# Where the last stage's weights are split: float32 kept during the attention, high and low halves made in the experts' stage

## The chip, the cores and the metric

One core of a Trainium2 chip runs the whole program in one launch. The metric is the device time of one execution in microseconds (us), the median of three runs. The engines are TensorE (PE, and PEld for its weight loads), VectorE (DVE), ScalarE (ACT), GpSimd (POOL), and SyncE (SP), which only issues DMAs.

## The reference

Three stages follow one another on 4 x 576 tokens of width 512:

```python
# 1. attention, 8 heads of 64, per batch
scores = scale * q @ k.T
scores = where(scores >= max(scores) - tau, scores, -1e9)
attn = exp(scores - max(scores)); attn /= sum(attn) + 1e-9
x = attn @ v                                   # heads side by side: 512 columns
# 2. experts: each token goes to one of 8 (fresh argmax, or that of the token before)
h = relu(x[b, s] @ w1[e])                      # w1: 8 x 512 x 1024
out[b, s] = p[e] * (h @ w2[e])                 # w2: 8 x 1024 x 512
# 3. feed-forward
xn = (x - mu) / sqrt(var + 1e-6) * g_ln
y = x + relu(xn @ w_ch1) @ w_ch2               # w_ch1: 512 x 2048, w_ch2: 2048 x 512
```

`w_ch1` and `w_ch2` come as float64. Products are wanted to float32 accuracy, and the kernel gets them from float16 matmuls: each operand is split into a high half (its float16 rounding) and a low half (what is left, in float16), and three products of halves are summed.

## The kernel before

**Order of the work.** Every engine takes its instructions in the order in which the code is written; nothing rearranges them. Waits between engines are semaphores, and an engine whose next instruction waits holds up all that stand behind it.

**Attention.** There are 16 pairs of heads with 9 items (row tiles of 128) each. Per item PE makes the scores (L399), DVE takes their maximum (L403), PE makes scores with the threshold added (L436, L441), ACT takes the exponential `e` (L446), DVE masks it into `em` (L452), ACT rounds the high half `hl` (L458), POOL subtracts to get the low half (L459), and PE multiplies by `v` (L474 to L478). Beside this, each pair's `q`, `k`, `v` are scaled and split (ACT L297, L305, L357, L362; POOL L306, L363), and POOL prepares the thresholds (L412 to L416). A table (`later`, filled by `at(item, step)`) puts background steps between the items.

**Weights of the last stage, first part.** Slots 0 to 10 of the 16 into which `w_ch1` and `w_ch2` are cut are converted during the attention, two halves (`a` = 0, 1) of 128 x 512 each, by `ffn_steps`. A half takes six steps at the offsets in `FO`: a DMA of the float64 words (L161), three DVE instructions that build the float32 (`narrow`, L142 to L146, into tile `cv`), a scaling on ACT (L164), and `low()`: ACT rounds the high half into `fw` (L157) and POOL subtracts for the low half (L158). `fw1` and `fw2` hold both halves for the whole program. Slots 11 to 15 are converted later by `ffn_half`, on ACT (L179) and DVE (L180).

**Experts.** The units are "a" and "b" (experts 0 and 1, two token tiles each), then 2 to 7 (two tiles of 128 tokens each), then 6 units whose expert is read from a register. A unit gathers its tokens (POOL, L904), transposes them (PE L987, ACT L988, DVE L989: tile `xT`), makes the hidden layer in four steps `k` (PE L1012, ACT L1016, DVE L1017: tile `hid`), then two output tiles (PE L1033, ACT L1039), and POOL scatters them (L1040, L1041). Between the steps `pace` runs the splits of the next unit's weights, eight chunks of 128 x 1024: high on ACT (L124), low on DVE (L125). In unit "b" DVE also makes the tables for the later units (L825 to L872, POOL L867).

**Feed-forward.** Nine groups of 256 tokens: PE L1144 and L1157 read `fw1` and `fw2`.

Of the kernel before, what the change touches and what calls it, by code (L numbers as in the profile page):

```python
# [8 lines left out]
F32 = mybir.dt.float32  # L9
# [3 lines left out]
AF = mybir.ActivationFunctionType  # L13
ALU = mybir.AluOpType
# [6 lines left out]
def kernel(  # L21
# [15 lines left out]
    nc = tc.nc  # L37
# [15 lines left out]
    def pool(c, name, bufs, **kw):  # L53
        return c.enter_context(tc.tile_pool(name=name, bufs=bufs, **kw))
# [65 lines left out]
    fw1 = fw_p.tile([128, 2, DM // 128, FF], F16, name="fw1")  # L120
    fw2 = fw_p.tile([128, 2, FF // 128, DM], F16, name="fw2")
# [5 lines left out]
    FA = 11  # L127

    def ffn_views(j):

        if j < 8:
            c, o = j // 2, 1024 * (j % 2)
            src = w_ch1[128 * c:128 * c + 128, o:o + 1024].rearrange("p (a b) -> p a b", a=2)
            return src, fw1[:, :, c, o:o + 1024].rearrange("p t (a b) -> p t a b", a=2), g32[:, c:c + 1]
        j -= 8
        src = w_ch2[256 * j:256 * j + 256, :].rearrange("(c p) f -> p c f", p=128)
        return src, fw2[:, :, 2 * j:2 * j + 2, :], 64.0

    def narrow(t, r):

        lo, hi = t[..., 0], t[..., 1]
        nc.vector.tensor_scalar(out=r, in0=hi, scalar1=3, scalar2=0x3FFFFFF8, op0=ALU.logical_shift_left, op1=ALU.bitwise_and)  # L142
        yield
        nc.vector.scalar_tensor_tensor(out=r, in0=hi, scalar=-(1 << 30), in1=r, op0=ALU.bitwise_and, op1=ALU.bitwise_or)
        yield
        nc.vector.scalar_tensor_tensor(out=r, in0=lo, scalar=29, in1=r, op0=ALU.logical_shift_right, op1=ALU.bitwise_or)  # L146
        yield

    def ffn_steps(j, a, cv_p):

        src, dst, scale = ffn_views(j)
        t = cv_p.tile([128, 512, 2], I32, name="stg")
        r = cv_p.tile([128, 512], I32, name="cv")
        rf = r.bitcast(F32)

        def low():
            nc.scalar.activation(out=dst[:, 0, a], in_=rf, func=AF.Copy)  # L157
            nc.gpsimd.tensor_tensor(out=dst[:, 1, a], in0=rf, in1=dst[:, 0, a], op=ALU.subtract)  # L158

        n = narrow(t, r)  # L160
        yield nc.sync.dma_start(out=t.rearrange("p b w -> p (b w)"), in_=src[:, a].bitcast(I32))  # L161
        for _ in range(3):
            yield next(n)
        yield nc.scalar.activation(out=rf, in_=rf, func=AF.Copy, scale=scale)  # L164
        yield low()

    def ffn_half(j, a):

# [15 lines left out]
    P, wt = {}, {}  # L184
# [45 lines left out]
    if True:  # L230
# [292 lines left out]
        def gate(p):  # L523

            b, hp = divmod(p, NP)
            xc = xcs[p]
            xt = xts[p % 2]
            ta = bank(b)
            for i in range(4):
                nc.tensor.transpose(ta[:, i, :], xc[:, i, :], ident)  # L530
            yield
            nc.scalar.activation(out=xt[:, 0:4, :], in_=ta, func=AF.Copy)
            close()
            yield
            tt = bank(b)
            nc.tensor.transpose(tt[:, 0, 0:64], xc[0:64, 4, :], ident[0:64, 0:64])
            yield
            nc.scalar.activation(out=xt[:, 4, 0:64], in_=tt[:, 0, 0:64], func=AF.Copy)
            close()
            yield  # L540
            lp = bank(b).rearrange("p a b -> p (a b)")[:, 0:80].rearrange("p (a b) -> p a b", b=16)
            for i in range(5):
                nc.tensor.matmul(lp[:, i, 0:9], xt[:, i, :], wg9[:, hp, :])
                if i % 2 and p < npair - 1:
                    yield
            yield
            lg = lgs[b % 2]
            if hp == 0:
                nc.vector.tensor_copy(out=lg, in_=lp[:, :, 0:9])
            else:  # L550
                nc.vector.tensor_tensor(out=lg, in0=lp[:, :, 0:9], in1=lg, op=ALU.add)
            close()
            if hp == NP - 1:
                if b < B - 1:
                    routes.append([route(b), None])
                else:
                    yield
                    yield from route(b)
# [177 lines left out]
        def at(k, f, *a):  # L736
            later.setdefault(max(-FIRST, k), []).append((f, a))
# [15 lines left out]
        for p in range(npair):  # L753
# [9 lines left out]
                at(9 * p + 10 + 4 * a, start_norm, p, a)  # L763
            at(9 * p + 15 + (4 if p == npair - 2 else 1 if p < npair - 2 else 0), store, p)
            at(9 * p + (17 if p < npair - 1 else 15), lambda p=p: bgp.append(gate(p)))
        FO = ((-4, 2, 3, 5, 5, 8), (0, 6, 9, 8, 8, 13))
        for w, slot in enumerate((0, 1, 2, 3, 4, 5, 7, 8, 9, 11, 12)):
            for a in range(2):
                g = []
                def st(w=w, a=a, g=g):  # L770
                    if not g: g.append(ffn_steps(w, a, cv_p))
                    next(g[0], None)
                for o in FO[a]:
                    at(max(-1, 9 * slot + o), st)
# [115 lines left out]
    def tiles(u):  # L890

        if u in PAIRS:
            return PAIRS[u]
        return (2 * u, 2 * u + 1) if u < E else (E + u,)

    def single(u):
        return u not in PAIRS and u >= E

    def gather(u):
        us[u, "g"] = []  # L900
        for n, c in enumerate(tiles(u)):
            xg = P["xgs"][u % 2 if single(u) else n]
            ix, R = (etb, NT - S) if u == "a" else (P["tb"], NT)
            nc.gpsimd.indirect_dma_start(  # L904
                out=xg[:], out_offset=None, in_=x_d[0:R, :], in_offset=bass.IndirectOffsetOnAxis(ap=ix[:, c:c + 1], axis=0),
                bounds_check=R - 1, oob_is_err=False)
            us[u, "g"].append(xg)
# [31 lines left out]
    def drip(n=1):  # L939

        if late:
            next(late.pop(), None)
        for _ in range(n):
            for k in pq:
                if k[0] == 1 and "wb_p" not in P:
                    return
                if k in parts and (not late if k[0] == "f" else k[0] < 2 or (k[0] - 2, k[1] // 4) in done):
                    break
                if k[0] != "f":
                    return  # L950
            else:
                return
            pq.remove(k)
            if k[0] == "f":
                late.append(parts.pop(k))
                next(late[0])
            else:
                parts.pop(k)()
            more()

    def pace(u, share):

        n = 0
        for k in pq:
            if k[0] != "f" and (k[0] - u) * 8 + k[1] > (7 if u < 6 else 11):
                break
            n += 1
        drip(int(n * share + 0.99))
# [8 lines left out]
    def new_x(u):  # L977
        us[u, "x"] = P["u_p"].tile([128, 2, 2, 4, 128], F16, name="xT")

    def t_unit(u):  # L980

        new_x(u)
        x = us[u, "x"]
        for n, xg in enumerate(us.pop((u, "g"))):
            t = P["pa"].tile([128, 4, 128], F32, name="a")
            for c in range(4):
                nc.tensor.transpose(t[:, c, :], xg[:, 128 * c:128 * c + 128], ident)  # L987
            nc.scalar.activation(out=x[:, 0, n], in_=t, func=AF.Copy, scale=64.0)  # L988
            V.scalar_tensor_tensor(out=x[:, 1, n], in0=t, scalar=64.0, in1=x[:, 0, n], op0=ALU.mult, op1=ALU.subtract)  # L989
# [55 lines left out]
    def s1_unit(u, k):  # L1045
        for _ in s1_steps(u, k):
            pass

    def s2_unit(u, i, between):
        for _ in s2_steps(u, i, between):  # L1050
            pass
# [18 lines left out]
    def f_load(g):  # L1070
        xf = P["f_p"].tile([128, 2, DM + 1], F32, name="xf", bufs=2)
        nc.sync.dma_start(out=xf, in_=ys_d[256 * g:256 * g + 256, :].rearrange("(t p) d -> p t d", p=128))
        fs[g] = xf
# [111 lines left out]
    with tc.manual_schedule():  # L1185
# [121 lines left out]
        for _ in ew: pass  # L1307
        t_unit("b")
        gather(2)
        for u in ["b"] + list(range(2, E)):  # L1310
            v = 1 if u == "b" else u
            for k in range(4):
                s1_unit(u, k)
                pace(v + 1, SH[k])
                for _ in range(3 if u == "b" else 1):
                    next(ut, None)
            t_unit(v + 1)
            gather(v + 2)
            if u == E - 1:
                gather(v + 3)  # L1320
            s2_unit(u, 0, lambda: pace(v + 1, SH[4]))
            if u == 2:
                dyn_tables()
                c_unit.close()
                c_tab.close()
                P["f_p"] = pool(ctx, "f", 1)
                P["f2_p"] = pool(ctx, "f2", 2)
            s2_unit(u, 1, lambda: pace(v + 1, SH[5]))
        f_load(0)
        for i in range(ND0):  # L1330
            u = E + i
# [76 lines left out]
```

## Time and profile before

| | |
|---|---|
| median of 3 runs | 1051.86 us (1051.25 to 1055.43) |
| the profiled execution | 1051.45 us, of which the span from first to last instruction is 1049.7 us |
| PE, DVE, ACT, POOL busy in the span | 990.2, 652.8, 505.1, 392.8 us |
| mean granted clock of PE | 0.988 |
| attention, pairs 1 to 14 | 54 to 376 us of the span |
| unit "b", unit 2, units 3 to 6 | 438 to 461, 461 to 484, 484 to 592 us |

Busy shares over the whole span mix stages with different limits, so each stage is read by itself: the windows table gives the busy time of every engine in a stretch. In the timeline a time in square brackets is the engine's idle time just before the instruction and what ended it; an instruction without brackets followed the one before it. A busy PE is not PE at its peak, since the ends of its matmuls are modelled.

### The profile page before, as it was taken

Reading aid. Unit: us, or ns where it says so; the run is one execution under the profiler, and the core shown is the slowest. Engines: PE = TensorE matmul, PEld = TensorE weight load, DVE = VectorE, ACT = ScalarE, POOL = GpSimd, SP = SyncE. Lnnn points to the kernel's source line nnn. Section 1 sums busy time; section 2 is a strip of 40 time slices with the busy share of each in tenths; the row PEclk is TensorE's granted clock in tenths of the full one; section 3 lists DMA queues with packets and bytes.
Section 4 is the critical chain, followed back from the end, with each engine's and each line's share of the span. In section 5 each row is a group of like instructions: output and inputs, shape, how many; then the busy total and the mean of one; then the engine's idle time right before and its main releaser. Section 6 shows DMA issues by size and latency. Waiting matters only on the chain. (4 is left out here: it accounts for less than half of the span.)

```text
span 1049.7 us, 23757 instructions
## 1 busy us (share of the span) xinstructions
PE 990.2 (94%) x9946; PEld 728.9 (69%) x9946; DVE 652.8 (62%) x1127; ACT 505.1 (48%) x791; POOL 392.8 (37%) x411
## 2 busy tenths in 40 slices
PE   6899998998999988899999999999999999999995
PEld 3678877787888776676667677594858668567572
DVE  7788888988897777797787777363324133131220
ACT  4688786786777666356566554242212011011010
POOL 3699897797788671334222211101000000000000
PEclk8999999999999999999999999999999999999998
DMA  7556544464442646668889775363111110111100
GB/s 179 138 133 166 132 103 126 112 156 119 113 108 47 166 153 213 214 217 278 268 290 304 239 251 164 105 200 106 38 31 40 52 32 31 54 28 41 31 11 23
DMA packets 122454, 136.83 MB, mean 130 GB/s; under 512 B 65370, under 2 KB 86874, under 8 KB 122336
## 3 DMA queue, kind: packets, MB, share of 16 engines
q1 hardware_dynamic: 98336, 116.43, 38.3%
q0 software_dynamic: 4960, 14.17, 3.7%
q10 hardware_dynamic: 19040, 4.61, 2.1%
q8 instruction: 80, 1.31, 0.5%
q14 instruction: 38, 0.31, 0.1%
HBM read 100.17 MB, written 19.94 MB: 114 GB/s over the span
## 5 line engine op out<-in xcount | busy, mean ns | idle before, releaser
L1144 PE MATMUL a<-nT,fw 128*128 128x256 f16 x1728 | 190.3, 273 | 0.8 <-DVE nT L1113 0.8
L459 POOL TENSOR_TENSOR hl<-em,hl 128x576 f16<-128x576 f32 x128 | 169.5, 1325 | 54.0 <-ACT hl L458 52.8
L1157 PE MATMUL y<-fw,hid 128*128 128x512 f16 x864 | 187.9, 379 | 0.0
L1144 PEld LDWEIGHTS <-fw 128*128 128x128 f16 x1728 | 169.1, 98 | 22.4 <-issue 0.9
L1157 PEld LDWEIGHTS <-hid 128*128 128x128 f16 x864 | 84.6, 98 | 100.4
L1147 ACT ACTIVATE hid<-a 128x512 f16<-128x512 f32 x72 | 42.7, 593 | 213.2 <-PE a L1144 211.3
L125 DVE SCALAR_TENSOR_TENSOR w<-stg,w 128x1024 f16<-128x1024 f32 x112 | 135.2, 1231 | 15.7 <-ACT w L124 14.8
L446 ACT ACTIVATE e<-s,t 128x576 f32<-128x576 f32 x144 | 106.0, 736 | 70.2 <-PE s L441 57.6
L1162 POOL DMA_INDIRECT out_dram<-xf x18 | 19.1, 1059 | 311.8 <-DVE xf L1161 311.8
L1012 PE MATMUL a<-xT,w 128*128 128x128 f16 (+1 forms) x1536 | 121.4, 241 | 1.4 <-DVE w L125 0.9
L1033 PE MATMUL y<-w,hid 128*128 128x512 f16 x528 | 117.8, 379 | 3.0 <-DVE hid L1017 2.7
L1012 PEld LDWEIGHTS <-w 128*128 128x128 f16 x1536 | 112.2, 99 | 11.1 <-DVE w L125 1.0
L403 DVE TENSOR_REDUCE mc<-sm 128x1 f32<-128x576 f32 x138 | 103.6, 751 | 24.7 <-PE sm L399 22.7
L124 ACT ACTIVATE w<-stg 128x1024 f16<-128x1024 f32 x112 | 114.4, 1051 | 6.1 <-DMA stg<-in_moe_w_dram 3.5
L452 DVE SCALAR_TENSOR_TENSOR em<-s,e 128x576 f32<-128x576 f32 x144 | 107.1, 745 | 9.7 <-POOL hl L459 8.5
L1148 DVE SCALAR_TENSOR_TENSOR hid<-a,hid 128x512 f16<-128x512 f32 x72 | 49.6, 688 | 98.9 <-ACT hid L1147 98.9
L1161 DVE SCALAR_TENSOR_TENSOR xf<-y,xf 128x512 f32<-128x512 f32 x18 | 12.5, 692 | 146.8 <-PE y L1157 146.8
L399 PE MATMUL sm<-qkt 128*128 128x288 f16 (+1 forms) x308 | 75.4, 291 | 24.3 <-DVE mc L403 21.4
L458 ACT ACTIVATE hl<-em 128x576 f16<-128x576 f32 x128 | 86.9, 679 | 18.8 <-DVE em L452 18.3
L1033 PEld LDWEIGHTS <-hid 128*128 128x128 f16 x528 | 51.0, 98 | 62.2 <-DVE hid L1017 4.5
L436 PE MATMUL s<-qkt 128*128 128x288 f16 (+1 forms) x320 | 90.2, 290 | 3.8 <-DVE em L452 3.1
L441 PE MATMUL s<-th,ind 128*128 128x128 bf16 (+5 forms) x960 | 91.9, 206 | 0.0
(295 smaller groups left out, 1800.4 us busy)
## 6 DMA issues: line engine op xcount, KB each, us to landing
stg<-in_moe_w_dram SPq DMA_DIRECT2D x112, 512.0 KB
stg<-in_moe_w_ch_dram SPq DMA_DIRECT2D x32, 512.0 KB
ys_d<-stg SPq DMA_DIRECT2D x6, 769.5 KB
xf<-ys_d SPq DMA_DIRECT2D x9, 513.0 KB
x_d<-xc SPq DMA_DIRECT2D x16, 256.0 KB
ku<-qkt SPq DMA_DIRECT2D x28, 144.0 KB
rawq<-in_q_dram SPq DMA_DIRECT2D x7, 512.0 KB
rawk<-in_k_dram SPq DMA_DIRECT2D x7, 512.0 KB
```

Of the source, the lines that this page charges most:

```text
L124: nc.scalar.activation(out=dst[:, 0, n], in_=t, func=AF.Copy, scale=scale)
L125: nc.vector.scalar_tensor_tensor(out=dst[:, 1, n], in0=t, scalar=scale, in1=dst[:, 0, n], op0=ALU.mult, op1=ALU.subtract)
L403: nc.vector.tensor_reduce(out=mcs[p % 2][:, j:j + 1], in_=mms.pop((p, j))[:, W0:W0 + 576], op=ALU.max, axis=AX.X)
L436: mm(o[:, W0 + 288 * c:W0 + 288 * c + 288], (kt, ku)[k][:, n], y, start=(k == 0), stop=False)
L441: mm(o[:, W0 + i:W0 + i + w], ind[:, t % 4, 0:o.shape[0]], y, start=False, stop=(i == of[-1][0]))
L446: nc.scalar.activation(out=e, in_=mst[p, j][:, W0:W0 + 576], func=AF.Exp, bias=t0, scale=SC)
L452: nc.vector.scalar_tensor_tensor(out=em, in0=ps[:, W0:W0 + 576], scalar=0.0, in1=e, op0=ALU.is_ge, op1=ALU.mult)
L459: nc.gpsimd.tensor_tensor(out=hl[:, 1], in0=em, in1=hl[:, 0], op=ALU.subtract)
L1012: nc.tensor.matmul(ps[:, f, :], t1[:, a, c, fc], x[:, h, i:i + N // 128, c, :], start=(n == 0), stop=(n == 11))
L1033: nc.tensor.matmul(ps, hid[:, x, f, 128 * i:128 * i + 128], t2[:, a, f, :], start=(n == 0), stop=(n == 23))
L1144: nc.tensor.matmul(ps[:, f, :], fw1[:, a, c, fc], x[:, h, :, c, :], start=(n == 0), stop=(n == 11))
L1157: nc.tensor.matmul(ps, hid[:, x, f, ts_], fw2[:, a, f, :], start=(n == 0), stop=(n == 47))
```

## The change

`low()` goes from the attention. ACT's scaling step (now L179 of the new file, L164 before) writes its float32 result to the bytes of `fw1` or `fw2` that the two halves will take: 512 float32 need as many bytes as 512 high and 512 low float16. In the experts' stage `ffn_finish` makes the halves of a slot in two parts: two copies on POOL into a float32 tile `f16`, then two roundings on ACT and two subtractions on POOL. One part is issued after each of the four hidden steps of units "b" and 2 to 7, until the 22 parts are done, which is in unit 6.

```diff
+    def ffn_whole(j, a):
+
+        c = j // 2
+        if j < 8:
+            o = 512 * (j % 2) + 256 * a
+            return fw1.bitcast(F32)[:, :, c, o:o + 256]
+        return fw2.bitcast(F32)[:, :, 2 * (j - 8) + a, :]
+
+    def ffn_finish(j):
+
+        dst = ffn_views(j)[1]
+        r = P["n_p"].tile([128, 2, 512], F32, name="f16", tag="f16")
+        for a in range(2):
+            nc.gpsimd.tensor_copy(out=r[:, a].rearrange("p (t f) -> p t f", t=2), in_=ffn_whole(j, a))
+        yield
+        for a in range(2):
+            nc.scalar.activation(out=dst[:, 0, a], in_=r[:, a], func=AF.Copy)
+        for a in range(2):
+            nc.gpsimd.tensor_tensor(out=dst[:, 1, a], in0=r[:, a], in1=dst[:, 0, a], op=ALU.subtract)
+        yield
+
     def ffn_steps(j, a, cv_p):
...
-        rf = r.bitcast(F32)
-
-        def low():
-            nc.scalar.activation(out=dst[:, 0, a], in_=rf, func=AF.Copy)
-            nc.gpsimd.tensor_tensor(out=dst[:, 1, a], in0=rf, in1=dst[:, 0, a], op=ALU.subtract)
-
+        rf = r.bitcast(F32).rearrange("p (t f) -> p t f", t=2)
         n = narrow(t, r)
         yield nc.sync.dma_start(out=t.rearrange("p b w -> p (b w)"), in_=src[:, a].bitcast(I32))
         for _ in range(3):
             yield next(n)
-        yield nc.scalar.activation(out=rf, in_=rf, func=AF.Copy, scale=scale)
-        yield low()
+        yield nc.scalar.activation(out=ffn_whole(j, a), in_=rf, func=AF.Copy, scale=scale)
...
-        FO = ((-4, 2, 3, 5, 5, 8), (0, 6, 9, 8, 8, 13))
+        FO = ((-4, 2, 3, 5, 5), (0, 6, 9, 8, 8))
...
         gather(2)
+        fin = (x for j in range(FA) for x in ffn_finish(j))
         for u in ["b"] + list(range(2, E)):
             v = 1 if u == "b" else u
             for k in range(4):
...
                 for _ in range(3 if u == "b" else 1):
                     next(ut, None)
+                next(fin, None)
             t_unit(v + 1)
...
+        for _ in fin: pass
         f_load(0)
```

On POOL in the attention, from the split of one pair's `v` (`vl`) to the split of the next pair's `q` (`nat`), before:

```order
L363 TENSOR_TENSOR vl_164<-vraw,vh_163 128x640
L459 TENSOR_TENSOR hl<-em,hl 128x576
L158 TENSOR_TENSOR fw_96<-cv,fw_96 128x512
L459 TENSOR_TENSOR hl<-em,hl 128x576
L459 TENSOR_TENSOR hlt<-em,hlt 128x576
L459 TENSOR_TENSOR hl<-em,hl 128x576
L306 TENSOR_TENSOR nat<-rawq,nat 128x9x64
```

The same stretch in the changed kernel, whose line numbers are 15 higher there:

```order
L378 TENSOR_TENSOR vl_164<-vraw,vh_163 128x640
L474 TENSOR_TENSOR hl<-em,hl 128x576 x2
L474 TENSOR_TENSOR hlt<-em,hlt 128x576
L474 TENSOR_TENSOR hl<-em,hl 128x576
L321 TENSOR_TENSOR nat<-rawq,nat 128x9x64
```

The subtraction into `fw` is gone, and all else keeps its place; it is so at all 22 places, and on ACT with the rounding L157. The order on PE, DVE and SP is the same in both kernels throughout.

On POOL from the gathers for unit 2 (`xg`) to the first output of unit "b" (`yb`), before:

```order
L904 DMA xg_7409<-x_d,tb 128x512
L904 DMA xg_7410<-x_d,tb 128x512
L867 TENSOR_TENSOR ova<-oca,val_79 128x1280
L904 DMA xg_7409<-x_d,tb 128x512
L904 DMA xg_7410<-x_d,tb 128x512
L1040 COPY yb<-tb 128x1
L1041 DMA ys_d<-yb,didx 2304x513
```

And in the changed kernel (`f_8461`, `f_8594` are the float32 tile `f16`):

```order
L919 DMA xg_7365<-x_d,tb 128x512
L919 DMA xg_7366<-x_d,tb 128x512
L162 COPY f_8461<-fw_96 128x512 x2
L167 TENSOR_TENSOR fw_96<-f_8461,fw_96 128x512 x2
L882 TENSOR_TENSOR ova<-oca,val_79 128x1280
L162 COPY f_8594<-fw_96 128x512 x2
L167 TENSOR_TENSOR fw_96<-f_8594,fw_96 128x512 x2
L919 DMA xg_7365<-x_d,tb 128x512
L919 DMA xg_7366<-x_d,tb 128x512
L1055 COPY yb<-tb 128x1
L1056 DMA ys_d<-yb,didx 2304x513
```

Four copies and four subtractions stand between the two pairs of gathers, around the table product `ova`; units 2 to 5 have the same eight ahead of their gathers, and unit 6 has four.

On ACT in unit 2, from the first to the last rounding of `hid`, before:

```order
L1016 ACTIVATE hid<-a 128x512
L179 ACTIVATE fw_97<-xn 128x512
L124 ACTIVATE w_8828<-stg 128x1024
L1016 ACTIVATE hid<-a 128x512
L124 ACTIVATE w_8828<-stg 128x1024
L1016 ACTIVATE hid<-a 128x512
L124 ACTIVATE w_8828<-stg 128x1024
L1016 ACTIVATE hid<-a 128x512
```

And in the changed kernel:

```order
L1031 ACTIVATE hid<-a 128x512
L194 ACTIVATE fw_97<-xn 128x512
L124 ACTIVATE w_8798<-stg 128x1024
L1031 ACTIVATE hid<-a 128x512
L124 ACTIVATE w_8798<-stg 128x1024
L165 ACTIVATE fw_96<-f_8803 128x512 x2
L1031 ACTIVATE hid<-a 128x512
L124 ACTIVATE w_8798<-stg 128x1024
L1031 ACTIVATE hid<-a 128x512
```

Two roundings into `fw` stand ahead of the third rounding of `hid`, and two more behind the last one's weight split.

## Rows read from the trace of the kernel before

**Rows 1.** Windows: window, its us, busy us (instructions) by engine, clock, DMA share.

```profile
54.00:376.00 322.00, 303.20 (x4417) 253.63 (x4414) 277.40 (x505) 244.16 (x414) 262.41 (x257) 0.99 0.50 125
...
438.00:461.00 23.00, 22.53 (x253) 16.73 (x253) 18.75 (x40) 11.07 (x15) 11.42 (x9) 1.00 0.42 131
461.00:484.00 23.00, 22.95 (x189) 15.87 (x187) 21.50 (x27) 13.54 (x18) 8.41 (x6) 1.00 0.91 305
484.00:592.00 108.00, 108.00 (x757) 74.33 (x756) 82.23 (x94) 67.92 (x89) 27.54 (x29) 1.00 0.85 278
```

**Rows 2.** Groups of instructions: shapes, count, busy us, mean ns, idle before.

```profile
L158 POOL TENSOR_TENSOR fw<-cv,fw 128x512 f16<-128x512 f32 x22 | 25.5, 1160 | 0.0
...
L157 ACT ACTIVATE fw<-cv 128x512 f16<-128x512 f32 x22 | 13.7, 624 | 0.0
```

**Rows 3.** Timeline, POOL, one pair of the attention: start, us.

```profile
129.39 1.16 POOL L158 TENSOR_TENSOR fw<-cv,fw 128x512 f16<-128x512 f32 x1
131.42 1.28 POOL L459 TENSOR_TENSOR hl<-em,hl 128x576 f16<-128x576 f32 x1 [0.87 <-ACT hl L458]
...
141.61 1.16 POOL L158 TENSOR_TENSOR fw<-cv,fw 128x512 f16<-128x512 f32 x1
142.73 1.27 POOL L459 TENSOR_TENSOR hl<-em,hl 128x576 f16<-128x576 f32 x1
144.16 1.28 POOL L459 TENSOR_TENSOR hlt<-em,hlt 128x576 f16<-128x576 f32 x1 [0.16 <-ACT hlt L458]
```

**Rows 4.** Timeline, ACT, the same pair.

```profile
127.98 0.62 ACT L157 ACTIVATE fw<-cv 128x512 f16<-128x512 f32 x1
130.03 0.74 ACT L446 ACTIVATE e<-s,t 128x576 f32<-128x576 f32 x1 [1.44 <-PE s L441]
...
138.22 0.64 ACT L157 ACTIVATE fw<-cv 128x512 f16<-128x512 f32 x1
139.55 0.74 ACT L446 ACTIVATE e<-s,t 128x576 f32<-128x576 f32 x1 [0.69 <-PE s L441]
```

**Rows 5.** Waits in 50 to 400 us: who for whom, us, times, longest.

```profile
DVE em L452 <- POOL hl L459: 8.5, 13, 1.9
```

**Rows 6.** Groups of instructions: a POOL instruction with no input.

```profile
L1269 POOL MEMSET xg<- 128x512 f32 x2 | 1.0, 522 | 0.0
```

**Rows 7.** Timeline, DVE, units "b" and 2.

```profile
442.94 0.69 DVE L1017 SCALAR_TENSOR_TENSOR hid<-a,hid 128x512 f16<-128x512 f32 x1 [3.81 <-ACT hid L1016]
...
451.58 3.70 DVE L872 TENSOR_TENSOR ola<-iota,lo_a 128x640 f16<-128x640 f32 x2
...
456.93 1.55 DVE L872 TENSOR_TENSOR ola<-iota,lo_a 128x640 f16<-128x640 f32 x2
...
459.60 5.75 DVE L125 SCALAR_TENSOR_TENSOR w<-stg,w 128x1024 f16<-128x1024 f32 x5
466.15 0.43 DVE L142 TENSOR_SCALAR xn<-stg 128x512 int32<-128x512 int32 x1 [0.80 <-DMA stg<-in_moe_w_ch_dram]
...
469.67 1.22 DVE L125 SCALAR_TENSOR_TENSOR w<-stg,w 128x1024 f16<-128x1024 f32 x1 [0.25 <-ACT w L124]
...
474.28 0.68 DVE L1017 SCALAR_TENSOR_TENSOR hid<-a,hid 128x512 f16<-128x512 f32 x1
```

**Rows 8.** Timeline, POOL, unit "b".

```profile
451.75 2.84 POOL L867 TENSOR_TENSOR ova<-oca,val 128x1280 f16<-128x1280 f16 x1 [10.06 <-DVE oca L865]
```

**Rows 9.** Groups of instructions: one DVE operation in the attention, then later.

```profile
L146 DVE SCALAR_TENSOR_TENSOR cv<-stg,cv 128x512 int32<-128x512 int32 x22 | 24.1, 1093 | 0.4
...
L146 DVE SCALAR_TENSOR_TENSOR xn<-stg,xn 128x512 int32<-128x512 int32 x10 | 6.9, 692 | 0.3
```

**Rows 10.** Timeline, PE, unit 2: hidden layer, then first output tile.

```profile
460.43 10.64 PE L1012 MATMUL a<-xT,w 128*128 128x256 f16 x96
...
472.05 5.13 PE L1033 MATMUL y<-w,hid 128*128 128x512 f16 x23
```

**Rows 11.** Timeline, ACT, unit 2: the last rounding of `hid`.

```profile
472.39 0.59 ACT L1016 ACTIVATE hid<-a 128x512 f16<-128x512 f32 x1
```

## The prediction, made before the changed kernel was run

> **What bounds the kernel now.** I read the windows by stage first, then the timelines of POOL and ACT around the instructions that go, then those of DVE, PE and ACT where new work comes in. In the attention four engines are nearly full: of 322 us DVE works 277, POOL 262, ACT 244, and PE is kept for 303 [rows 1]. So a lighter POOL and ACT could in principle shorten it; whether they do is read from the waits. In units 3 to 6 PE has no pause at all in 108 us, and in units "b" and 2 half a microsecond in 46 [rows 1]. There a later PE ends the program later, and nothing behind gives it back. In unit 2 DVE works 21.5 of 23 us [rows 1]: it is the engine with the least to spare just where the added work begins.
>
> **The attention: what goes.** 22 subtractions on POOL, 25.5 us, and 22 roundings on ACT, 13.7 us [rows 2]. To be worth something, each would have to be followed by work without a pause up to something another engine waits for. The timeline of a full pair shows the two patterns. On POOL the first subtraction (129.39) is followed by 0.87 us of idleness, for ACT's `hl`; the second (141.61) by one more `hl` without a pause, and then by 0.16 us of idleness, again for ACT [rows 3]. All 22 places are of these two kinds: thirteen have idle time right behind them (0.44 us or more), nine one instruction later (0.15 to 0.59 us). On ACT every one of the 22 is followed by a wait for PE's scores, 0.69 to 2.53 us; the two of this pair are 1.44 and 0.69 us [rows 4]. What is released earlier is thus one `hl` in every second case, and the next one still waits for ACT. In the whole attention DVE waited for POOL's `hl` 13 times, 8.5 us in all [rows 5]. Followed back on POOL, none of these 13 reaches a subtraction into `fw` before POOL was idle for ACT, and no PE wait does. So I value the removal at 0 us; the bounds are 0 and a gain of 8.5 us.
>
> The scaling on ACT stays, with another destination of as many bytes: nothing. DVE and SP have the same instructions in the same order.
>
> **The experts: what comes.** 22 copies and 22 subtractions on POOL and 22 roundings on ACT. A subtraction keeps its 1.16 us and a rounding its 0.62 us [rows 2]. A POOL copy of 128 x 512 float32 is not in the trace: from below it has the filling of such a tile, 0.52 us [rows 6], from above the two-input subtraction, 1.16 us. With one input I take 0.6 us, near the filling.
>
> POOL itself has room: it works 27.5 of 108 us in units 3 to 6 [rows 1]. Behind its new work stand the next unit's gathers and the scatters. The gathers for unit 3 go out some 3.5 us later, but their tokens are turned only after unit 2's hidden layer, at 460.43 + 10.64 = 471.1 us [rows 10], so they cost nothing. The last slot is finished in unit 6, before the feed-forward reads `fw`.
>
> What does cost is DVE. While POOL ran its one table product of 2.84 us [rows 8], two instructions of DVE took 3.70 us together that otherwise take 1.55: DVE stood still for 2.15 us [rows 7]. Throughout the attention, where POOL is busy, the same float32 assembly takes 1093 ns against 692 ns in the experts' stage [rows 9]. The Trainium skill (SBUF — State Buffer, section "SBUF: two separate sides") says why: VectorE and GpSimd share a pair of ports, and an instruction of VectorE with two SBUF inputs and one of GpSimd that reads SBUF lock each other out for a whole instruction. The 2.15 us agree with that. It is a rule against this change, because the low halves of the experts' weights on DVE read two tiles of SBUF.
>
> How much reaches PE is counted up to the tightest place, the end of unit 2's hidden layer. The first two copies are free: DVE idles until 442.94 [rows 7]. From there to the last `hid` of unit 2 (474.28) the order puts in six subtractions and four copies: 6 x 1.16 + 4 x 0.6 = 9.4 us of POOL. DVE's idle time there is 0.80 + 0.25 = 1.05 us [rows 7]. Eight of its instructions (six `hid`, two `xT`) read a matmul's result and not two tiles of SBUF; at 0.68 us each they are 5.4 us in which POOL may work beside them.
> - From below, all of that cover used: 9.4 - 1.05 - 5.4 = 2.9 us later.
> - From above, none of it used: 9.4 - 1.05 = 8.3 us later.
> - I take half of it: 5.6 us, since POOL's instructions are longer than `hid` and begin when ACT and the locks allow, not when DVE turns to a matmul's result.
>
> PE's slack: the second tile's matmuls are 5.13 / 23 = 0.22 us apart, the last `hid` is first needed by the 20th, at 472.05 + 19 x 0.22 = 476.2, and was ready at 474.28 + 0.68 = 475.0 us [rows 7, 10]: 1.2 us. The start of unit 2 is as tight: the fourth weight chunk, the first of five from 459.60 on [rows 7], ends at 460.8, and the 12th of 96 matmuls needs it at 460.43 + 11 x 0.11 = 461.6 us [rows 10]. A delay before it is the same delay, and not counted twice. PE loses 5.6 - 1.2 = 4.4 us, with bounds of 2.9 - 1.2 = 1.7 and 8.3 - 1.2 = 7.1 us.
>
> ACT's two roundings ahead of the third `hid` of unit 2 move the last one from 472.39 to 473.64, and its end to 474.23 us [rows 11]. DVE took it up at 474.28 [rows 7], so this alone is just hidden, by 0.05 us. If it were not, it would be 1.25 us inside the upper bound.
>
> Units 3 to 6 get 14 copies and 14 subtractions, 24.6 us, where DVE has 108 - 82.2 = 25.8 us free [rows 1]. I cost them at nothing, on the ground that weights there are wanted a unit later; the cover is thin, and a rival below prices its loss.
>
> **The sum.** Attention 0, units "b" and 2 +4.4, units 3 to 6 0. On the profiled execution, 1051.45 us (span 1049.7 and 1.75 around it), that is 1055.9. It lies 0.4 us under the median of the runs, so I say **1056.3 us**, 0.4% over 1051.86.
>
> **The rivals.**
> - *All hidden.* DVE, whose instructions stand ready one behind the other, keeps POOL waiting rather than the reverse, and POOL's work falls into later gaps. For it: nobody needs `fw` before the feed-forward. Against it: the 2.15 us for which DVE stood still [rows 7, 8]. PE loses 0 to 1 us: 1052.4 us.
> - *Full price.* Every microsecond of POOL work lands on DVE, because POOL's turn falls on a weight split each time. For it: DVE's 21.5 of 23 us [rows 1] leave hardly another place. 7.1 us: 1051.86 + 7.1 = 1059.0 us. This is the rule of the shared ports named above, at its hardest; the attention's 1093 against 692 ns [rows 9] bears out part of it.
> - *The loss goes on.* The 24.6 us of units 3 to 6 use up DVE's 25.8 us and the last `hid` is late in units 3, 4 and 5 as well, each by half of the 4.4 us: 1056.3 + 6.6 = 1062.9 us. Against it: the work is spread over a whole unit, in which DVE has about a quarter free [rows 1].
> - *The other side: the attention gets shorter.* With four engines near full, POOL's `hl` comes earlier everywhere, DVE's 8.5 us of waits [rows 5] vanish, and PE in the experts loses only 1.7 us: 1051.86 - 8.5 + 1.7 = 1045.1 us. It decides from the point at which those waits shrink by more than the experts lose. Against it: the idle time behind every removed instruction [rows 3, 4].
>
> **How the numbers follow.** Forecast 45%, with a range of its own from 1053.6 to 1058; all hidden 20%, full price 22%, the loss goes on 7%, the attention shorter 6%. Half a percent, about what a measurement can tell from no change, is 5.3 us, so slower begins at 1057.1. To slower go full price, the loss that goes on and about a quarter of the forecast: 22 + 7 + 11 = 40%. Faster, below 1046.6, is most of the last rival: 5%. The rest is 55%. A range from 1051.3 to 1061 us leaves out the shorter attention, a little of the hidden case and the far end of the two dear ones.
>
> **What would show it.** Right: pairs of the attention at the length they had, POOL and ACT with longer waits for `hl` and for PE's scores in the places of L158 and L157; in units "b" and 2 weight splits on DVE longer than their 1.2 us, new POOL subtractions longer than 1.16 us, a PE pause of 2 to 5 us before or in unit 2's hidden layer and another at its first output tile, and none in units 3 to 5. Wrong: a pair shorter by some tenths of a microsecond, so that DVE's waits for `hl` had hung on the load and not on ACT; no pause of PE in unit 2; or pauses that come again in each later unit.

## The result, and the profile after

The changed kernel takes 1065.66 us (median of 4 runs, 1064.9 to 1069.87), the kernel before 1052.34 beside it: a ratio of 1.013, with a 95% interval of 1.0114 to 1.0146. That is 13.3 us slower. The forecast was 1056.3 us, with a range up to 1061: the side was right, but the slowdown forecast was a third of the one measured.

The profiled execution took 1065.89 us (span 1064.1). The same stages as in [rows 1], later by what had been lost up to there: the attention, unit 2, units 3 to 6 (columns: window, its us, busy us of PE, PEld, DVE, ACT and POOL, granted clock, DMA share, GB/s):

```profile
54.00:376.00 322.00, 303.82 (x4406) 254.46 (x4404) 275.35 (x497) 232.72 (x392) 238.54 (x234) 0.99 0.50 124
464.00:492.00 28.00, 23.67 (x183) 16.17 (x183) 23.34 (x28) 18.87 (x26) 18.69 (x17) 0.94 0.73 239
494.00:586.00 92.00, 87.95 (x611) 59.52 (x609) 71.01 (x79) 61.73 (x86) 57.41 (x54) 1.00 0.78 265
```

The last row has no counterpart in [rows 1]. A unit's first matmul of the hidden layer marks its start; before, unit 3 begins at 484.17 us and unit 7 at 571.02. The window from 484 to 592 us, which the table and the prediction call units 3 to 6, is therefore units 3 to 7. Units 3 to 6 before:

```profile
484.00:571.00 87.00, 87.00 (x610) 59.90 (x609) 67.20 (x77) 55.59 (x73) 21.36 (x23) 1.00 0.85 282
```

In the attention POOL works 23.9 us less and ACT 11.4 us less than before, PE as much and DVE 2.0 us less. In unit 2 PE now stands still for 4.3 us, and in units 3 to 6 for 4.0 us; before, it hardly paused there.

The groups of the new work in the experts (count | busy us, mean ns | idle before, releaser), which answer to [rows 2, 6]:

```profile
L125 DVE SCALAR_TENSOR_TENSOR w<-stg,w 128x1024 f16<-128x1024 f32 x60 | 77.4, 1318 | 6.9 <-ACT w L124 6.0 <-issue 0.3
...
L167 POOL TENSOR_TENSOR fw<-f,fw 128x512 f16<-128x512 f32 x22 | 29.7, 1369 | 5.9 <-ACT fw L165 5.9
L162 POOL COPY f<-fw 128x512 f32<-128x512 f32 x22 | 17.2, 814 | 0.3
...
L165 ACT ACTIVATE fw<-f 128x512 f16<-128x512 f32 x22 | 13.0, 629 | 24.6 <-POOL f L162 24.6
```

The durations were right: a rounding takes 629 ns, and where nothing disturbs it a copy takes about 0.6 us (1.18 for two, below) and a subtraction 1.16. The means are longer because POOL and DVE hold each other up. What the prediction had not seen stands at the end of the last row: ACT, whose roundings were to be hidden, waits 24.6 us in all for POOL's copies.

**The attention.** The same pair as in [rows 4], on ACT:

```profile
130.67 0.74 ACT L461 ACTIVATE e<-s,t 128x576 f32<-128x576 f32 x1 [1.96 <-PE s L456]
...
140.19 0.74 ACT L461 ACTIVATE e<-s,t 128x576 f32<-128x576 f32 x1 [1.21 <-PE s L456]
```

and as in [rows 3], on POOL:

```profile
132.06 1.29 POOL L474 TENSOR_TENSOR hl<-em,hl 128x576 f16<-128x576 f32 x1 [1.99 <-ACT hl L473]
...
144.81 1.29 POOL L474 TENSOR_TENSOR hlt<-em,hlt 128x576 f16<-128x576 f32 x1 [1.28 <-ACT hlt L473]
```

Both waits of ACT grew by 0.52 us (from 1.44 and 0.69), both of POOL by 1.12 us (from 0.87 and 0.16): nearly all the time of the instruction that went (0.62 and 1.16 us) came back as waiting, and the items have their old distance. DVE's wait for POOL's `hl`, to be compared with [rows 5], did not move:

```profile
DVE em L467 <- POOL hl L474: 8.6, 13, 1.9
```

**Unit 2, the first pause.** DVE and POOL at the end of unit "b", where [rows 7, 8] had two `ola` in 1.55 us:

```profile
460.79 1.58 DVE L125 SCALAR_TENSOR_TENSOR w<-stg,w 128x1024 f16<-128x1024 f32 x1
462.29 3.47 DVE L887 TENSOR_TENSOR ola<-iota,lo_a 128x640 f16<-128x640 f32 x2
465.68 1.28 DVE L1004 SCALAR_TENSOR_TENSOR xT<-a,xT 128x512 f16<-128x512 f32 x2
466.88 5.75 DVE L125 SCALAR_TENSOR_TENSOR w<-stg,w 128x1024 f16<-128x1024 f32 x5
...
482.76 0.69 DVE L1032 SCALAR_TENSOR_TENSOR hid<-a,hid 128x512 f16<-128x512 f32 x1 [3.24 <-ACT hid L1031]
```

```profile
459.53 1.76 POOL L162 COPY f<-fw 128x512 f32<-128x512 f32 x2
461.54 3.54 POOL L167 TENSOR_TENSOR fw<-f,fw 128x512 f16<-128x512 f32 x2 [0.25 <-ACT fw L165]
465.22 1.46 POOL L919 DMA_INDIRECT xg<-x_d,tb  x1 [0.15 <-issue]
466.99 2.00 POOL L919 DMA_INDIRECT xg<-x_d,tb  x1 [0.31 <-issue]
...
469.55 1.73 POOL L1056 DMA_INDIRECT ys_d<-yb,didx  x1 [0.28 <-POOL yb L1055]
...
479.06 1.34 POOL L1056 DMA_INDIRECT ys_d<-yb,didx  x1 [7.52 <-DMA ys_d<-yb,didx]
480.39 1.18 POOL L162 COPY f<-fw 128x512 f32<-128x512 f32 x2
```

The two subtractions (3.54 us for 2 x 1.16) and the two `ola` (3.47 for 1.55) hold each other; `xT` is behind `ola` on DVE, and PE behind `xT`:

```profile
463.56 0.27 PE L1027 MATMUL a<-xT,w 128*128 128x256 f16 x1
467.01 12.20 PE L1027 MATMUL a<-xT,w 128*128 128x256 f16 x95 [3.17 <-DVE xT L1004]
...
483.51 1.47 PE L1048 MATMUL y<-w,hid 128*128 128x512 f16 x6 [0.34 <-DVE hid L1032]
485.85 1.25 PE L1048 MATMUL y<-w,hid 128*128 128x512 f16 x5 [0.87 <-DVE hid L1032]
```

After this pause the 95 matmuls take 12.20 us, against 10.64 for 96 in [rows 10]. The granted clock accounts for it: right behind the pause it is mostly at the lower of its two levels, 1.2 GHz, and 3 us at 0.54 with 9 us at 0.96 fall 1.7 us short of full speed:

```profile
467.00:470.00 3.00, 2.99 (x16) 2.11 (x16) 3.00 (x3) 1.81 (x3) 2.71 (x3) 0.54 0.51 131
470.00:479.00 9.00, 9.00 (x81) 7.94 (x80) 8.08 (x11) 3.71 (x5) 1.53 (x2) 0.96 1.02 355
```

**Unit 2, the second pause.** The POOL rows above show its start. The second scatter of unit "b" (479.06) waited 7.52 us until the first had landed, and the copies stand behind it. ACT in the same stretch:

```profile
460.76 1.19 ACT L165 ACTIVATE fw<-f 128x512 f16<-128x512 f32 x2 [6.70 <-POOL f L162]
...
481.06 1.18 ACT L165 ACTIVATE fw<-f 128x512 f16<-128x512 f32 x2 [3.10 <-POOL f L162]
482.15 0.58 ACT L1031 ACTIVATE hid<-a 128x512 f16<-128x512 f32 x1
```

ACT waits 3.10 us for a copy that nobody needs before the feed-forward; `hid`, which PE needs at once, is the next in its queue. From there come the row 482.76 of DVE and the two PE waits above. The same chain comes back in units 3, 4 and 5, where ACT waits 3.07, 4.30 and 4.72 us for the copies ahead of a `hid`, and the units are 0.0, 0.6 and 1.8 us longer than before: a wait of some 3 us is still covered there, and what is longer reaches PE. Over units "b" to 7 the sums of the waits are (who for whom: us, times, longest), first after, then the scatters' row of before:

```profile
POOL ys_d L1056 <- DMA ys_d<-yb,didx: 38.8, 6, 7.5
ACT fw L165 <- POOL f L162: 24.6, 10, 6.7
```

```profile
POOL ys_d L1041 <- DMA ys_d<-yb,didx: 12.8, 3, 4.4
```

So a scatter waited for the one before it already in the kernel before, up to 4.4 us; only there nothing stood behind it that another engine wanted soon.

**Unit 6 is another case.** Only one slot is left for it, and ACT waits 0.34 us for its copies. What is late there is the first `hid`, which ACT takes up 7.5 us behind the start of the unit (561.44), and before 4.0 us behind it (549.31). Ahead of it stands the conversion of a later slot's weights, `fw<-xn`, which waits for DVE. First after, then before:

```profile
563.92 0.63 ACT L194 ACTIVATE fw<-xn 128x512 f16<-128x512 f32 x1 [3.33 <-DVE xn L146]
...
568.98 0.59 ACT L1031 ACTIVATE hid<-a 128x512 f16<-128x512 f32 x1
```

```profile
553.27 0.59 ACT L1016 ACTIVATE hid<-a 128x512 f16<-128x512 f32 x1
```

DVE begins that conversion 0.6 us behind the start of the unit, and before 3.7 us ahead of it.

### The profile page after: what moved, and what is told of

It is laid out like the page before. It is cut to its first block, busy times and chain, and to the rows that moved or that the text cites. A ratio compares the mean times of both kernels' runs of the same rounds, so it can differ in the third digit from the quotient of the medians.

```text
span 1064.1 us, 23763 instructions
## 1 busy us (share of the span) xinstructions
PE 998.6 (94%) x9946; PEld 732.3 (69%) x9946; DVE 661.5 (62%) x1127; ACT 505.3 (47%) x791; POOL 419.3 (39%) x433
## 5 line engine op out<-in xcount | busy, mean ns | idle before, releaser
L125 DVE SCALAR_TENSOR_TENSOR w<-stg,w 128x1024 f16<-128x1024 f32 x112 | 141.0, 1284 | 14.4 <-ACT w L124 13.4
```

Source lines behind the costliest of these rows:

```text
L125: nc.vector.scalar_tensor_tensor(out=dst[:, 1, n], in0=t, scalar=scale, in1=dst[:, 0, n], op0=ALU.mult, op1=ALU.subtract)
```

## The experiments

Most runs are to tell apart two ways of losing time, called here the *place* (subtractions on POOL beside DVE's work that PE waits for) and the *queue* (copies behind a scatter, ACT behind the copies). The expectations call the first P and the second Q.

**The attention's part alone.** Nothing is finished in the experts' stage.

```diff
-        fin = (x for j in range(FA) for x in ffn_finish(j))
+        fin = iter(())
```

> The attention's part of the change alone: the float32 is left in the place of the halves and never split, and the scales are set to zero so that these bytes stay finite (the last stage's result is left out by that; its instructions are all there). Theory A (nothing in the attention waits for the removed instructions, and the 3.2 us by which the changed kernel's trace is behind at the start of the experts are intervals at the lower clock that come by chance): 1051 to 1054 us, no difference from before that can be measured. Rival B (the lighter ScalarE and GpSimd leave PE waiting in other places, and it loses its clock more often): about 1055.5 us. Rival C (the attention gains): under 1050 us.

Measured: 1052.49 us against 1052.04, ratio 1.001 (0.9993 to 1.0027). The removal gains nothing that can be measured.

**The experts' part alone**, added to the kernel before, with its results put into a scratch tile: `ffn_finish` of the change with the line below, and on POOL a product with that tile in place of the subtraction:

```diff
-            nc.scalar.activation(out=dst[:, 0, a], in_=r[:, a], func=AF.Copy)
+            nc.scalar.activation(out=scr[:, a], in_=r[:, a], func=AF.Copy, scale=0.0)
```

> The attention as before, halves made there, and the finishing work of the experts' stage added on top with its results thrown into a scratch tile (22 copies and 22 products on GpSimd, 22 roundings on ScalarE, in the changed kernel's places). Theory A: the whole loss is made here, 1062 to 1066 us. Rival B: about 3 us less than the changed kernel, 1062 to 1063 us. If the loss needed both parts together: near 1055 us.

Measured: 1065.48 us, ratio 1.0119 (1.0091 to 1.0146). As far as the intervals tell, the whole loss is made in the experts' stage.

**Without ACT's roundings** (the changed kernel; the high halves are not made).

```diff
-        for a in range(2):
-            nc.scalar.activation(out=dst[:, 0, a], in_=r[:, a], func=AF.Copy)
```

> The changed kernel without the 22 roundings on ScalarE (the high halves are left out, scales zero as in e1): GpSimd has all its copies and subtractions, so VectorE is held at the shared ports as before, but ScalarE no longer waits for GpSimd's queue. Theory Q (from unit 2's third step on PE is late because ScalarE's rounding waits for a copy that stands on GpSimd behind a scatter, and the next rounding of hid behind it): the pauses of units 4, 5, 6 (5.1 us in the trace) and that at unit 2's first output tile (1.9 us) go, the one at unit 2's start (5 us) stays: 1057 to 1060 us. Rival P (all of it is VectorE held by GpSimd): 1064 to 1066 us, all pauses still there.

Measured: 1062.06 us, ratio 1.0091 (1.0061 to 1.0121), between what the two theories asked for. ACT waits for no copy here, but the copies and subtractions now run one behind the other as soon as a scatter lets them, and hold DVE elsewhere: unit 5 alone is 4.4 us longer than before. Taking out one member of the chain changed when POOL works, so this run separates little.

**Copies ahead of the scatters.** All work is kept. Of the two slots of a unit, the first has its copies behind the gathers and ahead of the two scatters, and its roundings one step earlier; the second has its copies one step earlier, right behind the first slot's subtractions, and its roundings behind the unit's last `hid` as before.

```diff
+        next(fin)
...
-                next(fin, None)
+                if k != 2:
+                    next(fin, None)
             t_unit(v + 1)
             gather(v + 2)
+            next(fin, None)
```

> All the work of the changed kernel, but a slot's two copies on GpSimd are issued one place earlier, ahead of the two scatters of the unit (before the first output tile) for the first slot of a unit, and right behind the first slot's subtractions for the second. Theory Q: the copies are done long before ScalarE wants them, PE has no pause in units 4 to 6 and none at unit 2's first output tile: 1057 to 1060 us. Rival P: the same number of microseconds holds VectorE, 1064 to 1066 us.

Measured: 1059.42 us, ratio 1.008 (1.0053 to 1.0107): 0.5%, 5.3 us, of the loss went with the order alone, and the pauses in units 3 to 5 are gone. ACT still waits 2.4 to 4.3 us for the second slot's copies in units 2 to 5; but those roundings stand behind the unit's last `hid`, and in units 3 to 5 the wait costs nothing. What is left in unit 2 is the place: one weight split beside two subtractions, on DVE and on POOL, takes 3.74 us where it takes 1.22 in [rows 7] (a split of 3.75 us comes again in units 4 and 5, where PE loses nothing):

```profile
476.06 3.74 DVE L125 SCALAR_TENSOR_TENSOR w<-stg,w 128x1024 f16<-128x1024 f32 x1
```

```profile
476.42 2.29 POOL L167 TENSOR_TENSOR fw<-f,fw 128x512 f16<-128x512 f32 x2
```

**The same order, but from unit 3 on** (nothing is finished in units "b" and 2).

```diff
-                if k != 2:
+                if v > 2 and k != 2:
                     next(fin, None)
...
-            next(fin, None)
+            if v > 1:
+                next(fin, None)
```

> All the work, copies ahead of the scatters as in e4, but nothing is finished in units b and 2: the first slot's copies are issued at unit 2's gather, and the 11 slots fall into units 3 to 7 with the rest behind. Theory (unit 2 is the place with under 1.3 us to spare on VectorE, later units have several us): the 4.6 us that e4's trace lost in unit 2 go, 1053 to 1056 us. Rival (the loss belongs to the work and not to the place, it comes back in other units): 1058 to 1060 us.

Measured: 1055.71 us, ratio 1.0025 (1.0014 to 1.0037). Another 0.55%, 5.8 us, went with the place. What stays, 2.6 us by the medians, is lost in unit 6 (3.8 us in the profile).

**Without POOL's subtractions** (the changed kernel; the low halves are not made).

```diff
-        for a in range(2):
-            nc.gpsimd.tensor_tensor(out=dst[:, 1, a], in0=r[:, a], in1=dst[:, 0, a], op=ALU.subtract)
```

> The changed kernel without GpSimd's 22 subtractions (the low halves are left out, scales zero as in e1); copies and roundings at their places. Theory P+Q (at unit 2's start VectorE is held by the subtractions, later ScalarE waits for copies behind a scatter): the 5 us at unit 2's start shrink to 0 to 2, while the waits of ScalarE for copies and PE's pauses in units 2, 4, 5, 6 (about 7 us) stay in part: 1056 to 1060 us. Rival (VectorE's hold makes all of the loss): about 1053 us. Rival (the subtractions make none of it): 1065 us.

Measured: 1053.56 us, ratio 0.9999 (0.9979 to 1.002). My expectation was wrong: I had thought that the queue would go on costing time, since copies still stand behind scatters and roundings behind copies. The loss is gone altogether. On ACT and on POOL:

```profile
472.56 1.19 ACT L165 ACTIVATE fw<-f 128x512 f16<-128x512 f32 x2 [0.33 <-POOL f L162]
```

```profile
462.93 1.09 POOL L1054 DMA_INDIRECT ys_d<-yb,didx  x1 [2.19 <-issue]
...
470.69 1.00 POOL L1054 DMA_INDIRECT ys_d<-yb,didx  x1 [6.40 <-DMA ys_d<-yb,didx]
471.70 1.39 POOL L162 COPY f<-fw 128x512 f32<-128x512 f32 x2
```

The scatter waits for the landing here too (6.40 us), but the first one left at 462.93 and not at 469.55, since no subtractions held up the gathers and it. So the wait is nearly over when ACT comes to the rounding, and 0.33 us are left of 3.10; over units "b" to 7 ACT waits 7.0 us for copies and not 24.6. On this trace the queue costs time only because the subtractions push the scatters into the place where ACT wants the copies. The mean weight split on DVE takes 1270 ns in this kernel, 1220 before, 1318 after, and 1460 with the copies ahead of the scatters: how much DVE's instructions are lengthened in all does not set the loss, it depends on whether PE waits for them. That the copies, which read SBUF but have only one input, lengthen the splits of DVE as well (1270 ns against 1220) agrees with the lock that the Trainium skill describes (SBUF — State Buffer, section "SBUF: two separate sides"): any GpSimd instruction that reads SBUF against one of VectorE with two SBUF inputs.

**From unit 3 on, with the second roundings ahead of the last `hid`.** The parts are shifted by one step against the change. So a unit's first slot has its copies ahead of the scatters (and here of the gathers too) and the second behind them, as in the run from unit 3 on above. It is not the change's own order, in which both stand behind the scatters, though the expectation says so. What differs from the run above is mainly where the second slot's roundings stand on ACT, ahead of the unit's last `hid` and not behind it:

```diff
-                next(fin, None)
+                if v > 2 or v == 2 and k == 3:
+                    next(fin, None)
```

> The changed kernel with its own places for the parts, behind the scatters, but the first part is issued only at the end of unit 2. Queue theory: the subtractions push the gathers and with them the first scatter of a unit some 3.5 us later, the second scatter waits for its landing, the copies stand behind it and ScalarE's roundings wait for the copies 3 us or more in at least two of the units 3 to 6; the experts lose 4 to 6 us, 1057 to 1059 against 1052.9. Rival (all that the changed kernel loses is lost around unit 2, where VectorE is tightest, and the later pauses are its echo): no pause until unit 6, as with the copies ahead of the scatters from unit 3 on, 1054 to 1056.

Measured: 1058.92 us, ratio 1.0058 (1.0036 to 1.0081), in the range of the queue theory and 3.5 us above the run from unit 3 on above (the two intervals just touch). On ACT ahead of the last `hid` of units 4 and 5, and on POOL in unit 5:

```profile
519.94 1.19 ACT L165 ACTIVATE fw<-f 128x512 f16<-128x512 f32 x2 [2.73 <-POOL f L162]
...
543.90 1.18 ACT L165 ACTIVATE fw<-f 128x512 f16<-128x512 f32 x2 [4.52 <-POOL f L162]
```

```profile
539.00 1.00 POOL L1056 DMA_INDIRECT ys_d<-yb,didx  x1 [7.36 <-DMA ys_d<-yb,didx]
```

Behind the scatter of 539.00 stand the first slot's subtractions and then the second slot's copies. In units 3 to 6 only one of ACT's waits is above 3 us, not two as I had expected: 2.73 us in unit 4 cost PE nothing, 4.52 in unit 5 cost 1.6. That fits the changed kernel's 3.07, 4.30 and 4.72 us.

**The two subtractions apart** (the copies ahead of the scatters as above; the second subtraction of a slot is issued ahead of the next slot's copies). For the second slot of a unit the gathers now stand between its two subtractions. For the first slot nothing does, so on POOL they still run one behind the other.

```diff
-        for a in range(2):
-            nc.gpsimd.tensor_tensor(out=dst[:, 1, a], in0=r[:, a], in1=dst[:, 0, a], op=ALU.subtract)
+        nc.gpsimd.tensor_tensor(out=dst[:, 1, 0], in0=r[:, 0], in1=dst[:, 0, 0], op=ALU.subtract)
+        last = dst, r
```

> The kernel with the copies ahead of the scatters, but the two subtractions of a slot no longer stand one behind the other: the second is issued one part later, ahead of the next slot's copies. Theory that two subtractions in a row hold one VectorE instruction through both: the longest weight splits fall from 3.7 to about 2.5 us, the pause at unit 2's start from 2.8 to 1.5 us or less and that of unit 6 likewise, 1055.5 to 1057.5 against 1059.4. Rival (only the sum of the subtractions' time on the shared side counts): the same 11 subtractions by two cost the same, 1059 to 1060.

Measured: 1060.38 us, ratio 1.0076 (1.0056 to 1.0096). The time is as the rival said, but only half of the pairs were parted. In unit 2 the split of 3.74 us and the 1.8 us at the outputs are gone, but the five splits at the unit's start, 6.76 us before this edit and 5.75 in [rows 7], now take

```profile
462.32 7.43 DVE L125 SCALAR_TENSOR_TENSOR w<-stg,w 128x1024 f16<-128x1024 f32 x5
```

and units 3 to 5 lose 1.3 us where they had lost none. A split held through both subtractions is still there in units 3 to 5; on DVE and POOL in unit 3:

```profile
499.64 3.73 DVE L125 SCALAR_TENSOR_TENSOR w<-stg,w 128x1024 f16<-128x1024 f32 x1
```

```profile
500.00 1.18 POOL L174 TENSOR_TENSOR fw<-f,fw 128x512 f16<-128x512 f32 x1
501.12 1.17 POOL L161 TENSOR_TENSOR fw<-f,fw 128x512 f16<-128x512 f32 x1
```

So this run moved the loss and did not make it smaller; what all pairs apart would cost is not shown.

**A lighter VectorE in the attention** (the kernel before without the middle one of the three `narrow` instructions; the last stage's weights lose bits).

```diff
-        nc.vector.scalar_tensor_tensor(out=r, in0=hi, scalar=-(1 << 30), ...
+        if not skip: nc.vector.scalar_tensor_tensor(out=r, in0=hi, scalar=-(1 << 30), ...
```

> The kernel before, without one of the three VectorE instructions (the middle one, 22 in all, 21.8 us) that assemble the float32 in the attention, so that the last stage's first eleven weight slots have wrong values; all else as before. It takes about as much from VectorE in the attention as the change took from GpSimd (25.5 us). Theory (VectorE is what the attention's pairs wait for): 8 to 15 us faster, 1037 to 1044 us. Rival (the pairs are set by waits between PE and VectorE that no lighter engine shortens): under 3 us, 1049 to 1052 us.

Measured: 1054.27 us, ratio 1.0008 (0.999 to 1.0026). The attention's window, to be read against [rows 1]:

```profile
54.00:376.00 322.00, 303.91 (x4408) 254.34 (x4405) 251.69 (x483) 242.77 (x413) 252.42 (x255) 0.99 0.50 124
```

DVE works 25.7 us less and POOL 10 us less, and a pair takes 22.06 us against 22.09: the theory that the pairs wait for DVE's work falls. Not even the fullest engine sets the attention's time. ACT's waits for PE's scores, above, fit a chain from PE to DVE and ACT and back, item by item; no run tests that chain by itself.

**The copies by DMA** from SP's queue, so that ACT waits for no POOL instruction.

```diff
-            nc.gpsimd.tensor_copy(out=r[:, a]..., in_=ffn_whole(j, a))
+            nc.sync.dma_start(out=r[:, a]..., in_=ffn_whole(j, a))
```

> The changed kernel with its 22 copies made by DMAs from SyncE's queue instead of GpSimd, in the same places. Theory P+Q: ScalarE's roundings no longer wait behind a scatter and GpSimd holds VectorE for the subtractions only: PE's pauses in units 4 to 6 go and that at unit 2's start is smaller, 1055 to 1060 us. Rival (SyncE's queue stands behind loads that wait for a free buffer, and ScalarE waits for it instead): 1062 us or more.

Measured: 1093.15 us, ratio 1.0382 (1.0361 to 1.0402): the rival's side came true, and far dearer than expected. SP's row of one slot, and ACT's:

```profile
475.16 1.27 SPq L162 DMA_DIRECT2D f<-fw  x2
```

```profile
480.40 1.35 ACT L165 ACTIVATE fw<-f 128x512 f16<-128x512 f32 x2 [5.53 <-DMA f<-fw]
```

From the issue to the rounding it is 5.2 us, where two POOL copies took 1.2, and 3.9 to 5.7 us for the second to the ninth slot. So of ACT's 5.53 us only 0.3 lie ahead of the issue, where the rival looked for them; the rest lies between the issue and the landing. ACT's waits for `f` add up to 53.3 us (11 times), POOL's to 37.8. How much earlier SP's queue could have issued, and why the landing takes so long, was not separated.

The pauses of PE, place by place: how much longer than before each stretch is, from the first matmul of one stage to that of the next, in us, from one profile each ("roundings ahead" is the run with the second roundings ahead of the last `hid`):

| | changed | copies ahead | ahead, from unit 3 | roundings ahead, from unit 3 | subtractions apart | no subtractions |
|---|---|---|---|---|---|---|
| unit 2, hidden layer | 4.7 | 2.8 | 0.5 | -0.3 | 2.6 | 0.4 |
| unit 2, outputs | 1.8 | 1.8 | 0.0 | 0.0 | 0.0 | 0.0 |
| units 3 to 5 | 2.4 | 0.0 | 0.0 | 1.6 | 1.3 | 0.0 |
| unit 6 | 2.7 | 3.6 | 3.8 | 3.1 | 4.1 | 0.0 |
| units 7 to 13 | 0.3 | 0.2 | 0.0 | 1.0 | 0.0 | -0.1 |

## Why the prediction was wrong

- **The attention at 0: right.** In the pair shown, the waits behind the removed instructions grew by almost their own time, and the attention's part alone measures 1.001; a loss of up to 2.8 us is inside its interval. In the profile of after the experts begin 3.2 us late. With the same attention they begin between 0.2 us early (copies ahead of the scatters) and 2.4 us late (no roundings), 0.9 us late in the attention's part alone, and with the attention of before 4.0 us late (the experts' part alone). So this goes with the execution, and belongs to no step.
- **Durations: right** (copy 0.6, subtraction 1.16, rounding 0.62 us).
- **Units "b" and 2, +4.4 us (bounds 1.7 to 7.1): measured 4.7 + 1.8 = 6.6 us, inside the bounds, but not made of what the term was made of.** The pause of 3.17 us ahead of unit 2's hidden layer came as foretold, from a hold-up of DVE, though at the `ola` and `xT` and not at the fourth weight chunk. The lower clock behind it added 12.20 - 95 x 10.64 / 96 = 1.7 us, for which there was no term. The outputs' 1.8 us came through ACT's wait for the copies. The count of POOL's work was short by two copies as well: the second pair of unit 2 (484.17) also stands ahead of the last `hid`, which makes it six copies and the term 5.6 us. That the bounds held is in part luck.
- **"So they cost nothing", of the gathers, and units 3 to 6 "at nothing": this is the step that failed.** Measured 2.4 + 2.7 = 5.1 us, by two mechanisms. In units 3 to 5, 2.4 us, it is the queue. I asked of the gathers whether their tokens came in time, which they did, and not what stands behind them on POOL: the first scatter, the second, which waits until the first has landed, and now the next copies; and behind the copies, on another engine, the roundings, and behind those `hid`. With the order changed the 2.4 us are gone. The wait row of before, 12.8 us, could have been read for this. In unit 6, 2.7 us, it is not ACT's wait for the copies (0.34 us), and no order took the loss away. It went only with the subtractions. There DVE comes late to the conversion that stands ahead of the first `hid` on ACT.
- **The cover for that step was misread.** The 25.8 us of DVE's free time are those of units 3 to 7. In units 3 to 6 DVE had 87 - 67.2 = 19.8 us free, less than the 24.6 us of new POOL work: by its own sum the step had no cover. Yet DVE was not used up: after, it works 71.0 of 92 us there, only 3.8 us more than before, and has 21.0 us free. The sum asked how much free time there was, and the loss depended on what waited for what.
- **"Just hidden, by 0.05 us": wrong.** Two roundings were priced by their own 1.25 us. What they cost is what they wait for, 3.10 us here.
- **The rivals.** "The loss goes on" had nearly the right size (1062.9), at 7%, but by luck: it wanted DVE's free time used up and a loss in each of units 3 to 5, and half of what was lost behind unit 2 fell in unit 6. "All hidden", "full price" as the end of it, and the shorter attention did not come.

Terms corrected by the profile: 1051.45 + 6.6 + 5.1 + 0.3 = 1063.4 us. The median is 2.3 us above this; 0.9 of it is that the profiled execution of before lies so far under the median beside it, and the rest is not explained. The reordering gave back 5.3 us by the medians, but 3.6 by the pauses of the two profiles (1.9 in unit 2's hidden layer, 2.4 in units 3 to 5, and unit 6 lost 0.9 more).

Open: the landing wait of the scatters was not taken away by itself, so that the first scatter's lateness is the cause rests on the run without subtractions and on the trace. The run with the copies ahead moved roundings as well as copies, so how much each of the two moves gave is not shown. Unit 6 loses 2.7 to 4.1 us in every order tried; that the late conversion is the cause there is read from the trace, and nothing was run on that alone.

## What to carry to other kernels

Before work is moved to a queue that is half idle, look at what its idle time consists of: if an engine's instruction waits there for a transfer to land, everything put behind it inherits the wait, and so does every engine that is made to wait for it. Work that nobody needs soon must not stand, in an in-order queue, ahead of work that is needed at once, unless all that it waits for is already done. When free time is set against new work, check that both cover the same stretch. And time freed in a chain that goes to and fro between engines can come back as waiting, whichever engine looks full.

## What the runs showed of the hardware

- One DVE split with two SBUF inputs was held through two POOL subtractions in a row: 3.74 us instead of 1.22 (copies ahead of the scatters, units 2, 4 and 5). Two DVE `ola` and two subtractions issued together took 3.47 and 3.54 us, against 1.55 and 2.3 alone.
- Behind a PE pause of 3.17 us the granted clock read 0.54 over the next 3 us; behind one of 1.36 us, in the kernel with the copies ahead, it read 1.00 and 95 matmuls took 10.78 us, hardly more than the 10.53 that 95 took before.
- A scatter into `ys_d` waited up to 7.5 us for the scatter before it, while the two write the rows of different tokens.
- Copies of 256 KB within SBUF by DMA, issued beside the weight loads, had landed, two together, 4 to 6 us after the first issue; POOL needs 0.6 us for one.
